# Three unread products ahead of the second half, and the scaled C moved ahead of a scan: a fused scan and gated feed-forward kernel on one core

## The chip, the cores and the metric

The kernel runs on 1 core of a Trainium2 chip. The metric is the device time of one execution in microseconds; medians of several executions are quoted. The engines are called by their short names: PE is TensorE (matmuls), PEld its weight loads, DVE is VectorE, ACT is ScalarE, POOL is GpSimd, SP issues the transfers. The span of a profile is about 1.7 us shorter than the time of the same execution.

## The reference, cut to what matters

The first half is a chunked linear recurrence over a sequence (4 sequences, 8 heads, 768 positions, head size 32, state size 16); the second multiplies its result (3072 x 256) by a matrix, applies h * cos(h), and multiplies by another.

```
y_intra = einsum('bhij,bhjd->bhid', (C @ B^T) * L, x)        # L: products of a, from j to i
y_inter = einsum('bhin,bhnd->bhid', C, state) * decay_to_i
state   = decay_full * state + sum_j (B_j x_j) * decay_from_j
...
h = x @ w_in ;  g = h * cos(h) ;  out = g @ w_out            # 256 -> 2048 -> 256
```

The weights arrive as 64-bit floats and are made into 32-bit floats in 16 pieces on the chip. Everything is computed in 32 bits.

## The kernel before

The sequence is cut into 6 blocks of 128 positions. One iteration n of the main loop handles one of 16 slices f of the feed-forward layer for one block c: `first(n)` makes hp (two matmuls of 128x512), ACT and DVE make k, w, the cosine and gT from it, `second(n-2)` adds four products into o. The scan of the next block is spread over the same iterations, one sequence b every three: `turn` transposes B and C, `intra` makes the products g and masks them with lam into m, `finish` makes y and the new state. Each matmul of the program stands in the trace as two instructions (hp: 384 for 192 calls), so hp is an x4 there and one unread product an x2. (1, 0) means block c = 1, sequence b = 0. In block 0's iterations the weights' conversion is there as well (`grade`, `join`), so block 1's scan, which runs beside it, is the most crowded part for DVE.

```python
def pair(name):                      # two buffers, passed round: tp, g, g, y, s_ps, ...
    return psum.tile([P, 2, 4 * P], FP32, tag="scan", bufs=2, name=name)

def decays(c, b, t):                 # lam: one scan of 128x512 per half t
    ...
    V.tensor_tensor_scan(out=lam[c, b][:, hs]..., data0=rows_, data1=unit, ...)
    if t == 0:
        return
    if c > 0:
        reach[c, b] = r = scan.tile([P, P], FP32, tag="reach", bufs=2, name="reach")
        V.tensor_tensor_scan(out=r, data0=along[c][:, b], data1=ones, initial=1.0, ...)
    ...
    G.tensor_tensor(out=sc, ...)     # POOL

def turn(c, b, tag=None):
    ...                              # PE: transposes of B and C into tp
    for t in range(2):
        ACT.activation(cT[:, t], tp[:, 1], AF.Copy, scale=slot[:, t:t + 1])
    ACT.copy(out=bcT[:, 0], in_=tp[:, 0])
    if c > 0:                        # the scaled C: last reader of tp
        V.tensor_tensor(out=bcT[:, 1], in0=tp[:, 1], in1=reach[c, b], op=ALU.mult)

def finish(c, b, tag=None, fills=0):
    ...
    fill(y[:, 2:4], fills)           # products of ones that nothing reads
    ...
def join(which, i):                  # last steps of a weight piece
    V.tensor_scalar(out=bits, ...)
    V.scalar_tensor_tensor(out=bits, in0=high, ..., in1=bits, ...)
    G.tensor_tensor(out=dst, in0=bits, in1=last, op=ALU.add)   # POOL, two inputs
...
    # in the loop, for the next block's sequence b:
    if j == 0:
        decays(c + 1, b, 1)          # lam's second half, reach
    (turn, intra, finish)[j](c + 1, b)
```

Of the kernel before, what the change touches and what calls it, by code (L numbers as in the profile page):

```python
# [8 lines left out]
FP32 = mybir.dt.float32  # L9
# [3 lines left out]
ALU = mybir.AluOpType  # L13
# [12 lines left out]
def kernel(  # L26
# [23 lines left out]
    V, ACT, G, PE = nc.vector, nc.scalar, nc.gpsimd, nc.tensor  # L50
# [3 lines left out]
    P = 128  # L54
    NC = S // P
# [13 lines left out]
    scan = ctx.enter_context(tc.tile_pool(name="scan", bufs=2))  # L69
# [9 lines left out]
    def bank(shape, name, tag):  # L79
        return psum.tile(shape, FP32, tag=tag, bufs=2, name=name)  # L80

    def pair(name):

        return psum.tile([P, 2, 4 * P], FP32, tag="scan", bufs=2, name=name)


    raw, arow, along = {}, {}, {}
    ones = const.tile([P, P], FP32, name="ones")
    V.memset(ones, 1.0)

    def fill(dst, times=1):

        for _ in range(times):
            PE.matmul(dst, lhsT=ones, rhs=ones.unsqueeze(1).to_broadcast([P, dst.shape[1], P]),
                      start=True, stop=True, skip_group_check=True)
# [27 lines left out]
    def load_along(c):  # L123
# [11 lines left out]
        out=a_in, in_=a.rearrange("(u b) h (c p) -> (b h c) u p", u=NU, p=P))  # L135
# [25 lines left out]
    def grade(which, i, later=False):  # L161



        t = words.pop((which, i), None)
        if t is None:
            return
        low, high = t[:, :, 0], t[:, :, 1]
        mag = conv.tile([P, 2 * WC], FP32, tag="mag", bufs=3, name="mag")
        ACT.activation(mag, high.bitcast(FP32), AF.Abs)  # L170
        G.tensor_scalar(out=mag, in0=mag, scalar1=MOST, scalar2=LEAST,  # L171
                        op0=ALU.min, op1=ALU.max)
        last = conv.tile([P, 2 * WC], U32, tag="last", bufs=3, name="last")
        held[which, i] = (high, mag.bitcast(U32), last)

        def rest():
            ACT.activation(last, low, AF.Copy, scale=2.0 ** -29)
        if later:
            return rest
        rest()  # L180

    def join(which, i):



        if (which, i) not in held:
            return
        high, bits, last = held.pop((which, i))
        V.tensor_scalar(out=bits, in0=bits, scalar1=3, scalar2=0x3FFFFFFF,  # L189
                        op0=ALU.logical_shift_left, op1=ALU.bitwise_and)  # L190
        V.scalar_tensor_tensor(out=bits, in0=high, scalar=0xC0000000, in1=bits,  # L191
                               op0=ALU.bitwise_and, op1=ALU.bitwise_or)
        dst = kept(which, i)
        k = dst.shape[1]
        G.tensor_tensor(out=dst.bitcast(U32), in0=bits.rearrange("p (k f) -> p k f", k=k),
                        in1=last.rearrange("p (k f) -> p k f", k=k), op=ALU.add)
# [3 lines left out]
    for n in (0, 2, 1, 3, 4, 5):  # L200
# [14 lines left out]
                    fill=0.0, base=0, channel_multiplier=1)  # L215
    G.affine_select(out=own, in_=own, pattern=[[N, H], [0, D]], compare_op=ALU.is_ge,
                    fill=0.0, base=N - 1, channel_multiplier=-1)
# [18 lines left out]
    scaled, lam, reach, state, part, yT = {}, {}, {}, {}, {}, {}  # L236

    def heads(b):
        return slice(b * H, (b + 1) * H)
# [3 lines left out]
    def spread_a(b, tags):  # L243
# [3 lines left out]
        for t in range(2):  # L247
# [4 lines left out]
                          rhs=cut[:, u], start=(h == 0), stop=True, skip_group_check=True)  # L252
            spread[b].append(a_ps)

    def decays(c, b, t):


        if t == 0:
            lam[c, b] = scan.tile([P, H, P], FP32, tag="lam", bufs=3, name="lam")
        hs = slice(t * HH, (t + 1) * HH)  # L260
        rows_ = spread[b][t] if c == 0 else arow[c, b][:, hs]
        V.tensor_tensor_scan(  # L262
            out=lam[c, b][:, hs].rearrange("p h i -> p (h i)"),
            data0=rows_.rearrange("p h i -> p (h i)"),
            data1=unit.rearrange("p h i -> p (h i)"), initial=0.0,
            op0=ALU.mult, op1=ALU.add)
        if t == 0:
            return
        if c > 0:
            reach[c, b] = r = scan.tile([P, P], FP32, tag="reach", bufs=2, name="reach")  # L270
            V.tensor_tensor_scan(out=r, data0=along[c][:, b], data1=ones, initial=1.0,
                                 op0=ALU.mult, op1=ALU.mult)
        if c == NC - 1:
            return

        scaled[c, b] = sc = scan.tile([P, H, N], FP32, tag="sc", bufs=NB, name="sc")
        G.tensor_tensor(out=sc, in0=raw[c][0][:, 0, heads(b)],  # L277
                        in1=lam[c, b][:, :, P - 1:P].to_broadcast([P, H, N]), op=ALU.mult)
# [33 lines left out]
    def finish(c, b, tag=None, fills=0):  # L312
        (bcT, m), xr = part.pop((c, b)), raw[c][1]
        y = (pair("y")[:, 0] if tag is None else bank([P, 4 * P], "y", tag)
             ).rearrange("p (k i) -> p k i", k=4)
        fill(y[:, 2:4], fills)
        y = y[:, 0:2]
        if c > 0:
            s = state[c - 1, b].rearrange("p h d -> p (h d)")
            for t in range(2):  # L320
                PE.matmul(y[:, t], lhsT=s[:, t * P:(t + 1) * P], rhs=bcT[:, 1],  # L321
                          start=(t == 0), stop=False, skip_group_check=True)
        for h in range(H):
            q, t = h % 4, h // 4
            PE.matmul(y[32 * q:32 * q + 32, t], lhsT=xr[:, b, h], rhs=m[:, h],  # L325
                      start=(c == 0 and t == 0), stop=True, tile_position=(0, 32 * q),
                      skip_group_check=True)
        if b == 0:
            yT[c] = two.tile([P, 2, TB], FP32, tag="yT", name="yT")
        ACT.copy(out=yT[c][:, :, b * P:(b + 1) * P], in_=y)  # L330
        if c > 0:
            carry(c, b)

    def carry(c, b):

        if c == NC - 1:
            return
        xr, sc = raw[c][1], scaled.pop((c, b))
        s_ps = pair("s_ps")[:, 0, 0:2 * D]
        for q in range(4):  # L340
            two_ = slice(2 * q, 2 * q + 2)
            PE.matmul(s_ps[32 * q:32 * q + 32], lhsT=sc[:, two_].rearrange("p h n -> p (h n)"),  # L342
                      rhs=xr[:, b, two_].rearrange("p h d -> p (h d)"), start=True, stop=True,
                      tile_position=(0, 32 * q), skip_group_check=True)
        state[c, b] = new = states.tile([P, H, D], FP32, tag="state", name="state")
        by_two = "p (k t) d -> p k (t d)"
        V.tensor_tensor(out=new.rearrange(by_two, k=HP),
                        in0=s_ps.unsqueeze(1).to_broadcast([P, HP, 2 * D]),
                        in1=own.rearrange(by_two, k=HP), op=ALU.mult)
        if c > 0:  # L350
            V.scalar_tensor_tensor(out=new, in0=state.pop((c - 1, b)),
                                   scalar=reach[c, b][:, P - 1:P], in1=new,
                                   op0=ALU.mult, op1=ALU.add)


    hp, turns, gT, o = {}, {}, {}, {}
# [14 lines left out]
    def gate(n):  # L371
        cos = turns.pop(n)
        ACT.activation(cos, cos, AF.Sin, bias=quarter, scale=TWO_PI)  # L373
        gT[n] = ffn.tile([P, TB], FP32, tag="gT", bufs=LAG + 1, name="gT")
        V.tensor_tensor(out=gT[n], in0=hp.pop(n), in1=cos, op=ALU.mult)  # L375
# [26 lines left out]
    fill(bank([P, 4, P], "warm", "o"), 2)  # L402
    spread_a(0, ("h", "h"))
    decays(0, 0, 0)
    decays(0, 0, 1)
    spread_a(1, ("o", "o"))
    turn(0, 0)
# [19 lines left out]
    finish(0, 2, "o", 1)  # L427
    intra(0, 3)
    grade(*order[1])
    finish(0, 3, "o")  # L430
    join(*order[2])
    join(*order[1])
    load(1)
# [9 lines left out]
    for n in range(NC * NF + LAG):  # L443
        c, f = divmod(n, NF)
        rest = None
        if n < NC * NF:
            if f == 0 and c > 0:
                load(c + 2)
            first(n)
            if n + 3 < len(order):  # L450
                rest = grade(*order[n + 3], later=True)
            if n + 2 < len(order):
                join(*order[n + 2])
            gate(n)
            if rest:
                rest()
        if n >= LAG:
            second(n - LAG)
        if n < NB:
            carry(0, n)  # L460
        if c + 1 < NC:
            b, j = divmod(f - 3, 3)
            if 0 <= b < NB:
                if j == 0:
                    decays(c + 1, b, 1)
                (turn, intra, finish)[j](c + 1, b)
            b, j = divmod(f - 2, 3)
            if 0 <= b < NB and j == 0:
                decays(c + 1, b, 0)
            if f == NF - 1:  # L470
                raw.pop(c + 1)
                load_a(c + 2)
                load_along(c + 2)
# [30 lines left out]
```

## Time and profile before

| | before |
|---|---|
| time, median of 5 | 414.45 us (413.12 to 414.99) |
| span of the profile | 413.0 us |
| PE busy | 403.4 us (98%) |
| DVE busy | 269.7 us (65%) |
| ACT, POOL busy | 174.6, 42.8 us |
| granted clock, mean | 0.995 |

The table hides two things. The mean clock of 0.995 comes of one stretch of 3.4 us at half rate (0.50 from 23.05 to 26.46 us), and of 0.9 us more at the end of the span (0.50 from 412.17 us on), behind the last matmul. And 98% for PE is a count of time in which some matmul is in flight, so g counts as busy for all of its 1.34 us in block 1, though it takes 0.71 in block 2 and the rest is its second half waiting for a buffer. In the lines that follow, "L303" is line 303 of the kernel, and the lines of the changed kernel are one lower.

### The profile page before, as it was taken

The page shows a single profiled execution, that of the slowest core. Times are in us where ns is not written, and L with a number is a line of the kernel's source. Part 1 is how long each engine was busy: PE and PEld are TensorE (multiplying, and loading weights), DVE is VectorE, ACT ScalarE, POOL GpSimd, SP SyncE. Part 2 cuts the span into 40 slices and gives each one's busy share as a digit, 9 for nine tenths or more (in the row PEclk, how much of TensorE's full clock was granted, in tenths as well). Part 3 has the DMA queues.
Part 4 walks back from the last instruction along what each step waited for, and adds up shares of the span by engine and source line. Part 5 has one row for each costly group of instructions (what it writes and reads, how often), then busy time and mean ns, then how long its engine had stood idle before and what let it go on. Part 6 is the DMA issues. An engine that isn't in the chain of part 4 may idle for free.

```text
span 413.0 us, 5500 instructions
## 1 busy us (share of the span) xinstructions
PE 403.4 (98%) x2088; PEld 263.4 (64%) x2088; DVE 269.7 (65%) x410; ACT 174.6 (42%) x329; POOL 42.8 (10%) x62
## 2 busy tenths in 40 slices
PE   8979999999999999999999999999999999999995
PEld 5636665666666666666666666667666666666664
DVE  5979999964777664676764667674576664444442
ACT  2457575634344334443343433433443443433331
POOL 2265455410000000000000000000000000000000
PEclk9989999999999999999999999999999999999999
DMA  7999994092110164201146111120100000100001
GB/s 92 312 146 305 389 148 141 2 160 70 52 51 2 51 116 64 97 6 51 52 94 86 51 52 51 51 60 19 52 0 2 0 0 2 51 0 2 0 0 52
DMA packets 105978, 30.27 MB, mean 73 GB/s; under 512 B 75168, under 2 KB 101856, under 8 KB 105952
## 3 DMA queue, kind: packets, MB, share of 16 engines
q1 hardware_dynamic: 105952, 29.92, 30.7%
q8 instruction: 16, 0.26, 0.3%
q14 instruction: 10, 0.08, 0.1%
HBM read 26.57 MB, written 3.34 MB: 72 GB/s over the span
## 4 chain that ended last, share of the span: by engine, by line
PE 89%; SPq 5%; DVE 3%; DMA 2%; issue 0%; ACT 0%; DVEq 0%
PE hp L362 40%; PE o L386 39%; SPq L112 4%; PE g L303 4%; PE y L325 3%; PE y L321 2%; DMA words<-in_moe_w_in_dram 1%; DMA along<-a_all 1%; DVE mag L191 1%; PE tp L284 1%; PE tp L285 1%; DVE lam L262 0%; DVE mag L189 0%; PE s_ps L342 0%; DVE gT L375 0%
## 5 line engine op out<-in xcount | busy, mean ns | idle before, releaser
L362 PE MATMUL hp<-yT,w_in 128*128 128x512 f32 x384 | 186.6, 609 | 1.2 <-ACT yT L330 0.6
L386 PEld LDWEIGHTS o<-w_out,gT 128*128 128x128 f32 x768 | 145.9, 190 | 60.0 <-issue 44.0
L386 PE MATMUL o<-w_out,gT 128*128 128x256 f32 x768 | 181.1, 379 | 0.0
L366 ACT ACTIVATE k<-hp 128x512 int32<-128x512 f32 x96 | 57.3, 597 | 129.9 <-PE hp L362 129.9
L375 DVE TENSOR_TENSOR gT<-hp,w 128x512 f32<-128x512 f32 x96 | 66.2, 690 | 65.4 <-ACT w L373 65.4
L368 DVE SCALAR_TENSOR_TENSOR w<-hp,k 128x512 f32<-128x512 f32 x96 | 66.1, 689 | 63.0 <-ACT k L366 62.3
L362 PEld LDWEIGHTS hp<-yT,w_in 128*128 128x128 f32 x384 | 68.3, 191 | 58.7 <-issue 54.3
L373 ACT ACTIVATE w<-w,quarter 128x512 f32<-128x512 f32 x96 | 69.3, 722 | 76.3 <-DVE w L368 76.3
L262 DVE TENSOR_TENSOR_SCAN lam<-arow,unit 128x512 f32<-128x512 f32 x40 | 51.4, 1286 | 0.0
L307 DVE TENSOR_TENSOR m<-g,lam 128x512 f32<-128x512 f32 x48 | 30.7, 680 | 0.7 <-PE g L303 0.6
L277 POOL TENSOR_TENSOR sc<-bc,lam 128x128 f32<-128x128 f32 x20 | 8.2, 412 | 201.5 <-DVE lam L262 200.2
L303 PE MATMUL g<-cT,bcT 32*128 32x256 f32 x192 | 19.7, 426 | 1.9 <-ACT bcT L291 1.2
L289 ACT ACTIVATE cT<-tp,slot 128x128 f32<-128x128 f32 x48 | 14.6, 355 | 11.0 <-PE tp L285 11.0
L325 PE MATMUL y<-m,xr 128*32 128x128 f32 x384 | 15.9, 279 | 1.1 <-DVE m L307 1.1
L303 PEld LDWEIGHTS g<-cT,bcT 32*128 32x128 f32 x192 | 8.6, 183 | 10.8 <-issue 6.2
L191 DVE SCALAR_TENSOR_TENSOR mag<-words,mag 128x512 uint32<-128x512 uint32 x16 | 14.3, 894 | 0.5
L330 ACT COPY yT<-y 128x256 f32<-128x256 f32 x24 | 9.0, 374 | 11.6 <-PE y L325 11.5
L171 POOL TENSOR_SCALAR mag<-mag 128x512 f32<-128x512 f32 x16 | 12.2, 759 | 16.3 <-ACT mag L170 16.3
L321 PEld LDWEIGHTS y<-bcT,state 128*128 128x128 f32 x80 | 12.1, 191 | 1.0
L325 PEld LDWEIGHTS y<-m,xr 128*32 128x32 f32 x384 | 8.9, 109 | 5.3 <-DVE m L307 2.4
L321 PE MATMUL y<-bcT,state 128*128 128x128 f32 x80 | 12.2, 274 | 0.0
L170 ACT ACTIVATE mag<-words 128x512 f32<-128x512 f32 x16 | 10.8, 677 | 2.1 <-DMA words<-in_moe_w_in_dram 2.1
(43 smaller groups left out, 152.1 us busy)
## 6 DMA issues: line engine op xcount, KB each, us to landing
arow<-a_cut SPq DMA_DIRECT2D x20, 512.0 KB
words<-in_moe_w_in_dram SPq DMA_DIRECT2D x8, 512.0 KB
words<-in_moe_w_out_dram SPq DMA_DIRECT2D x8, 512.0 KB
xr<-in_x_dram SPq DMA_DIRECT2D x5, 512.0 KB
out_dram<-ob SPq DMA_DIRECT2D x10, 256.0 KB
bc<-in_B_dram SPq DMA_DIRECT2D x5, 256.0 KB
bc<-in_C_dram SPq DMA_DIRECT2D x5, 256.0 KB
along<-a_all SPq DMA_DIRECT2D x20, 64.0 KB
```

The source lines that it names most:

```text
L191: V.scalar_tensor_tensor(out=bits, in0=high, scalar=0xC0000000, in1=bits, op0=ALU.bitwise_and, op1=ALU.bitwise_or)
L262: V.tensor_tensor_scan(out=lam[c, b][:, hs].rearrange("p h i -> p (h i)"), data0=rows_.rearrange("p h i -> p (h i)"), data1=unit.rearrange ...
L303: PE.matmul(g[u // 2][:, u % 2, 0:2 * P], lhsT=bcT[r, 0], rhs=cT[r].rearrange("p t i -> p (t i)"), start=True, stop=True)
L307: V.tensor_tensor(out=m[:, hs].rearrange("p (k t) i -> p k (t i)", k=2), in0=g[u][:, :, 0:2 * P], in1=l[:, hs].rearrange("p (k t) i -> p k ...
L321: PE.matmul(y[:, t], lhsT=s[:, t * P:(t + 1) * P], rhs=bcT[:, 1], start=(t == 0), stop=False, skip_group_check=True)
L325: PE.matmul(y[32 * q:32 * q + 32, t], lhsT=xr[:, b, h], rhs=m[:, h], start=(c == 0 and t == 0), stop=True, tile_position=(0, 32 * q), skip ...
L362: PE.matmul(hp[n], lhsT=w_in[:, k, f * P:(f + 1) * P], rhs=yT[c][:, k], start=(k == 0), stop=(k == KT - 1))
L366: ACT.activation(k, hp[n], AF.Copy, bias=0.25, scale=INV_2PI)
L368: V.scalar_tensor_tensor(out=w, in0=hp[n], scalar=INV_2PI, in1=k, op0=ALU.mult, op1=ALU.subtract)
L373: ACT.activation(cos, cos, AF.Sin, bias=quarter, scale=TWO_PI)
L375: V.tensor_tensor(out=gT[n], in0=hp.pop(n), in1=cos, op=ALU.mult)
L386: PE.matmul(o[c][b // 2][:, b % 2], lhsT=g[:, b * P:(b + 1) * P], rhs=w_out[:, f], start=(f == 0 and (last or b % 2 == 0)), stop=(f == NF ...
```

## The change

It aims at both: more work for PE around the last y of block 0, so that its clock, 0.50 there for 3.4 us, is not lowered just ahead of the main loop, and the scaled C earlier on DVE, so that the products g find their buffer free. reach, which the scaled C needs, is made in the iteration before.

```diff
+    def reaches(c, b):
+        reach[c, b] = r = scan.tile([P, P], FP32, tag="reach", bufs=2, name="reach")
+        V.tensor_tensor_scan(out=r, data0=along[c][:, b], data1=ones, initial=1.0, ...)
     def decays(c, b, t):
...
-        if c > 0:
-            reach[c, b] = ...            # moved to reaches()
...
-    finish(0, 3, "o")
+    finish(0, 3, "o", 2)
+    fill(pair("warm")[:, 0, 0:2 * P].rearrange("p (k i) -> p k i", k=2), 1)
...
             if 0 <= b < NB:
+                (turn, intra, finish)[j](c + 1, b)
                 if j == 0:
                     decays(c + 1, b, 1)
-                (turn, intra, finish)[j](c + 1, b)
             b, j = divmod(f - 2, 3)
             if 0 <= b < NB and j == 0:
+                reaches(c + 1, b)
                 decays(c + 1, b, 0)
```

More of the change, by code (lines that the diff above doesn't have):

```diff
@@ L253, in spread_a @@
             spread[b].append(a_ps)
+    def reaches(c, b):
+        reach[c, b] = r = scan.tile([P, P], FP32, tag="reach", bufs=2, name="reach")
+        V.tensor_tensor_scan(out=r, data0=along[c][:, b], data1=ones, initial=1.0,
+                             op0=ALU.mult, op1=ALU.mult)
     def decays(c, b, t):
@@ L266, in decays @@
             op0=ALU.mult, op1=ALU.add)
-        if t == 0:
-            return
-        if c > 0:
-            reach[c, b] = r = scan.tile([P, P], FP32, tag="reach", bufs=2, name="reach")
-            V.tensor_tensor_scan(out=r, data0=along[c][:, b], data1=ones, initial=1.0,
-                                 op0=ALU.mult, op1=ALU.mult)
-        if c == NC - 1:
+        if t == 0 or c == NC - 1:
             return
```

## The prediction

That the clock would hold rests on the estimate from two windows of the profile before, one with PE busy 2.03 of 3.41 us (60%) ahead of the drop and one with 2.63 of 3.42 us (77%) without one. The 0.43 us of one unread product is an estimate as well, from o's products in the same trace: eight instructions of 128x256, two to a product, take 1.73 us from their first start to that of the next instruction (45.22 to 46.95 us) and 1.89 us to their own end.

> **What bounds the kernel now.** I read the page first, then the stretches of time, then the timeline and the landings of the transfers in the first 90 us. On the page PE is busy 403.4 of 413.0 us, and its tenths show where the rest is: a ramp at the start and a short tail.
>
> ```profile
> PE   8979999999999999999999999999999999999995
> PEclk9989999999999999999999999999999999999999
> ```
>
> The third digit of the clock row, an 8, is the first thing the change aims at. The matmul timeline around it (start, duration, engine, line, shape, in brackets the idle time before and its releaser):
>
> ```profile
> 20.23 0.71 PE L303 MATMUL g<-cT,bcT 32*128 32x256 f32 x8
> 21.72 0.42 PE L325 MATMUL y<-m,xr 128*32 128x128 f32 x8 [0.78 <-DVE m L307]
> 22.32 0.43 PE L325 MATMUL y<-m,xr 128*32 128x128 f32 x8 [0.17 <-DVE m L307]
> 23.32 3.51 PE L362 MATMUL hp<-yT,w_in 128*128 128x512 f32 x4 [0.58 <-ACT yT L330]
> 27.01 1.98 PE L362 MATMUL hp<-yT,w_in 128*128 128x512 f32 x4
> ```
>
> The last y of block 0 stands between idle times of 0.78, 0.17 and 0.58 us, and the first product of the second half (hp, n = 0) then takes 3.51 us where the next takes 1.98. The granted clock is 0.80 in 20 to 25 us and 0.85 in 25 to 30 us, that is (0.20 + 0.15) * 5 / 0.5 = 3.5 us at half rate.
>
> The second thing is hidden: PE counts as busy from 29.8 us on, but not all of that is work. Stretches of one scan step (three n) in block 1 and in block 2 (columns: PE, PEld, DVE, ACT, POOL busy, clock, DMA share, GB/s):
>
> ```profile
> 43.40:56.75 13.35, 13.35 (x76) 8.64 (x75) 13.11 (x21) 8.44 (x17) 6.54 (x7) 1.00 1.12 307
> 56.75:70.10 13.35, 13.35 (x76) 8.64 (x75) 13.11 (x21) 8.45 (x17) 6.56 (x7) 1.00 0.57 126
> 70.10:83.45 13.35, 13.35 (x76) 8.64 (x74) 13.11 (x21) 7.87 (x16) 5.97 (x6) 1.00 0.14 38
> 109.95:122.67 12.72, 12.72 (x79) 8.35 (x75) 9.12 (x14) 4.80 (x11) 0.41 (x1) 1.00 0.14 43
> ```
>
> The same matmuls take 13.35 us in block 1 and 12.72 us in block 2. In block 1 DVE is busy 13.11 of 13.35 us, since the weights' joins run beside the scan. The 0.63 us stand in one place, the g products:
>
> ```profile
> 53.44 1.91 DVE L262 TENSOR_TENSOR_SCAN lam<-arow,unit 128x512 f32<-128x512 f32 x1
> 55.28 0.39 DVE L271 TENSOR_TENSOR_SCAN reach<-along,ones 128x128 f32<-128x128 f32 x1
> 55.48 1.34 PE L303 MATMUL g<-cT,bcT 32*128 32x256 f32 x8
> 55.77 0.29 DVE L293 TENSOR_TENSOR bcT<-tp,reach 128x128 f32<-128x128 f32 x1
> ```
>
> g takes 1.34 us here and 0.71 in block 2. Its second half needs the PSUM pair of tp (two buffers, passed round), whose last reader is the scaled C (bcT), which stands behind lam and reach on DVE. For b = 0 it is worse: g's halves start at 41.38 and 42.77 us, and the next hp at 43.40 instead of 41.38 + 0.65 = 42.03, a loss of 1.37. From block 2 on PE has no hole; DVE has 3.6 us to spare per step.
>
> [...] here the longest gap is 0.78, and the drop followed a window (19.59 to 23.00) with PE busy only 2.03 of 3.41 us, while 2.63 of 3.42 (9.35 to 12.77) kept the clock. [...] lam from arow takes 1.21 us alone and 1.91 when w_in's last join on POOL (53.00 to 54.27) overlaps it; the join on DVE 0.69 or 0.98. [...]
>
> **The change part by part.** In block 0 it adds three unread products of 256 columns: two ahead of the last y, one behind. One takes about 0.43 us of the array (the existing ones: 0.60 with latency). The first two fill 20.94 to 21.80, and m is ready at 21.62, so they cost at most 0.1; the third lies in the 0.58 us in which PE waits for ACT's yT. Cost on the path about 0. Busy time in the window rises from 2.03 to about 3.2 of 3.41, so the clock should hold, and hp (n = 0) ends 1.6 us sooner (3.51 - 1.9). Through k (ACT 0.60), w (DVE 0.69), sin (ACT 0.72) and gT (DVE 0.69) that reaches the third hp, which waited for gT at 29.82: about 28.2 now.
>
> In the loop, no instruction is added or removed, four stand elsewhere: scaled C (0.29) goes ahead of lam's second half (1.21 to 1.91) and no longer right behind reach, and reach (0.39) moves to the step before. What I get by placing the measured durations one after the other:
> - The copies of a for (1, 0) land at 35.36 us and the seventh weight piece at 37.08, by the landings in the trace; neither depends on compute. lam's first half started at 35.87 and can start at 35.4 at the earliest: DVE gains only 0.45 there, not 1.6. sin (n = 3) stands behind the seventh piece's first step on ACT (37.17 to 37.85).
> - That lam then misses most of the POOL join that lengthened it to 1.59, and the other half likewise; so w (n = 4) comes at about 41.5, not 42.63. DVE gains 1.1.
> - Scaled C also waits for ACT's copy of the same tile, which ends at about 40.0 (last 0.67, cT 0.60, bcT 0.27 after sin). So g starts at about 40.05 in one piece, not at 41.38 in two, and the next hp at 40.8, not 43.40.
> - The y of (1, 0) then waits for m, at about 45.0 (46.17 before): hp (n = 6) at 45.8, not 48.17. PE gains 2.3 to 2.5.
> - For b = 1 to 3, PE can gain 0.63 more each, up to 2.5 + 1.9 = 4.4. But it must not outrun DVE: before, m was done 1.3 to 1.5 us before y needed it. With DVE ahead by 1.1 the limit is 2.6. DVE gains a little per step: lam's second half now comes after ACT's copy, when the POOL join is nearly over (up to 0.6 saved), the bubble of 0.1 between reach and scaled C is gone; against this it waits up to 0.4 for ACT, and reach pushes lam's first half into the next POOL operation (0.3). I take 0 to 0.5 per step, hence a limit at b = 3 between 2.6 and 4.1.
>
> Blocks 2 to 5: PE has no hole to fill. In the step with reach DVE is 0.39 us later, but gT has over 2 us of slack before hp needs its bank. Nothing there.
>
> Sum: 2.6 to 4.1, middle 3.3. 414.45 - 3.3 = 411.15; I say 411.2.
>
> **Rivals.**
> A: DVE is the bound of block 1 and gives nothing but order. Its instructions are the same, 13.11 of 13.35 us busy, so only the initial slack of 1.5 us is gained, and the hole reappears at y (waiting for m). For it: the busy share. Against: part of those 13.11 us is time blocked by POOL, which the new order avoids. Time: 412.5 to 413.
> B: The clock does not hold, or drops one or two windows later. For it: once hp (n = 1) ends at 27.1, PE waits until 28.2 for gT, 1.1 us in the window of 26.4 to 29.8: 68% busy, between the two shares seen. Against: most of that loss falls where transfers hold DVE anyway (35.36 and 37.08 us). It costs 0 to 1: 411.2 to 412.2.
> C: Everything is hidden: transfers set when block 1 begins. For it: the landings. Against: holes of 1.37 + 3 * 0.63 = 3.26 us in g come from DVE's order, not from a transfer. Time: 414.
> D: PE takes all it can (1.6 + 3.26 less a short wait for ACT): 4.4, giving 410.0.
> E: The wait of scaled C for ACT holds up DVE in all 20 steps and slows blocks 2 to 5. For it: the built program has that wait, and lam no longer covers it. Against: DVE is busy only 9.12 of 12.72 us there. Time if it did: 413 to 415.
>
> **Range and chances.** The middle is 411.2. A and B together pull towards 412.5, D towards 410.2; I put 8 in 10 on 410.2 to 412.7. Faster by over 2% would be below 406.2, more than every hole of PE after 20 us together; slower by over 2% would need over 8 us of new waits. So within 2% is nearly certain.
>
> **What would show it right or wrong.** The clock row should have no 8 in its third digit and the first hp should take about 1.98 us. The g products of block 1 should take about 0.71 us each, g of (1, 0) starting near 40 us, and a step of block 1 between 12.7 and 13.1 us. lam's second half should mostly take less than 1.9 us. Block 2's step should stay at 12.72 us; if it is longer, E holds. If block 1's step stays near 13.3 with the wait now at y, A holds. If g of (1, 0) still starts after 41 us, the transfers or the clock have taken the gain and my working from 35 us on is wrong.

## The result, and the profile after

The changed kernel takes 410.12 us (median of 5, 409.48 to 410.62) against 414.45. The ratio is 0.990, with a 95% interval of 0.988 to 0.992. Ratios here are the mean time of one kernel's fast executions over that of the other's in the same rounds, so not quite the ratio of the medians; in the last call of the experiments, 11 of the 12 executions of the kernel before are those of the first call, on the same chip. The gain of 4.3 us is clear of the noise. The median lies 0.08 us under the low end of the predicted range.

The tenths of PE's busy time and of its clock, 40 slices of the span, after:

```profile
PE   8999999999999999999999999999999999999995
PEclk9999999999999999999999999999999999999999
```

The 7 (PE) and the 8 (clock) of the third slice are gone. The matmul timeline around block 0's last y, after:

```profile
20.57 0.71 PE L302 MATMUL g<-cT,bcT 32*128 32x256 f32 x8
21.21 1.13 PE L94 MATMUL y<-ones 128*128 128x256 f32 x4
22.27 0.81 PE L324 MATMUL y<-m,xr 128*32 128x128 f32 x16
23.02 0.70 PE L94 MATMUL warm<-ones 128*128 128x256 f32 x2
23.67 1.95 PE L361 MATMUL hp<-yT,w_in 128*128 128x512 f32 x4
25.80 1.98 PE L361 MATMUL hp<-yT,w_in 128*128 128x512 f32 x4
28.61 1.96 PE L361 MATMUL hp<-yT,w_in 128*128 128x512 f32 x4 [0.57 <-DVE gT L374]
```

The unread products stand where PE waited, nothing else moved for them, and the first hp takes 1.95 us. From g to hp it is 3.10 us (20.57 to 23.67), before 3.09 (20.23 to 23.32), so they cost nothing. The third hp still waits 0.57 us for gT, but it starts at 28.61, not 29.82.

The steps of block 1 and one of block 2, after (columns: PE, PEld, DVE, ACT, POOL busy with the number of instructions, clock, DMA share, GB/s):

```profile
40.82:53.54 12.72, 12.72 (x78) 8.36 (x74) 12.22 (x22) 8.20 (x16) 6.54 (x7) 1.00 1.13 358
53.54:66.26 12.72, 12.72 (x78) 8.36 (x74) 12.23 (x21) 8.20 (x16) 6.47 (x8) 1.00 0.83 148
66.26:78.98 12.72, 12.72 (x78) 8.36 (x74) 12.21 (x21) 7.64 (x15) 6.45 (x8) 1.00 0.14 43
105.48:118.20 12.72, 12.72 (x79) 8.35 (x75) 9.11 (x15) 5.00 (x10) 0.41 (x1) 1.00 0.14 42
```

A step of block 1 now takes exactly what one of block 2 takes, 12.72 us. DVE is busy 0.9 us less per step (12.22, was 13.11) with the same instructions. Where the 0.9 went is seen in the timeline of the step of b = 1, after:

```profile
51.12 1.27 POOL L195 TENSOR_TENSOR w_in<-mag,last 128x512 uint32<-128x512 uint32 x1 [1.32 <-DVE mag L191]
51.99 0.29 DVE L292 TENSOR_TENSOR bcT<-tp,reach 128x128 f32<-128x128 f32 x1 [0.36 <-ACT bcT L290]
52.20 1.27 DVE L267 TENSOR_TENSOR_SCAN lam<-arow,unit 128x512 f32<-128x512 f32 x1
52.90 0.71 PE L302 MATMUL g<-cT,bcT 32*128 32x256 f32 x8
```

The scaled C waits 0.36 us for ACT's copy, lam starts when POOL's join (51.12 to 52.39) is nearly over and takes 1.27 us instead of 1.91, and g finds its buffer free.

The ledger, from the starts of hp in the two traces:

| stretch | before | after | gain |
|---|---|---|---|
| start to hp of n = 0 | 23.32 | 23.67 | -0.35 |
| n = 0 to n = 1 (clock) | 3.69 | 2.13 | 1.56 |
| n = 4 to n = 5 (g of b = 0) | 5.56 | 4.18 | 1.38 |
| n = 7 to 8, 10 to 11, 13 to 14 (g of b = 1 to 3), each | 4.81 | 4.18 | 0.63 |
| sum of the last three rows, the last of them taken three times | | | 4.83 |

With the later start the net is 4.5 us; the spans differ by 4.4 (413.0 and 408.6). The later start lies ahead of anything that was changed.

The chain that ended last says the same by engine, first before, then after:

```profile
PE 89%; SPq 5%; DVE 3%; DMA 2%; issue 0%; ACT 0%; DVEq 0%
```

```profile
PE 97%; ACT 1%; DVE 1%; issue 0%; DVEq 0%
```

Before, the chain left PE at g of (1, 0) and ran back over DVE to the transfers; after, it is PE nearly all the way.

### The profile page after: what moved, and what is told of

The parts are those of the page before. It is cut to its first block, busy times and chain, and to the rows that moved or that the text cites. A ratio compares the mean times of both kernels' runs of the same rounds, so it can differ in the third digit from the quotient of the medians.

```text
span 408.6 us, 5540 instructions
## 1 busy us (share of the span) xinstructions
PE 401.1 (98%) x2094; PEld 263.1 (64%) x2094; DVE 266.7 (65%) x410; ACT 173.8 (43%) x329; POOL 42.3 (10%) x62
## 4 chain that ended last, share of the span: by engine, by line
PE 97%; ACT 1%; DVE 1%; issue 0%; DVEq 0%
PE hp L361 42%; PE o L385 41%; PE g L302 4%; PE y L324 3%; PE y L320 2%; PE a_ps L251 2%; PE warm L94 1%; PE tp L283 1%; PE tp L284 1%; PE s_ps L341 1%; PE y L94 0%; ACT cT L288 0%; ACT w L372 0%; DVE m L306 0%; DVE gT L374 0%
## 5 line engine op out<-in xcount | busy, mean ns | idle before, releaser
L267 DVE TENSOR_TENSOR_SCAN lam<-arow,unit 128x512 f32<-128x512 f32 x40 | 48.6, 1214 | 0.0
L302 PE MATMUL g<-cT,bcT 32*128 32x256 f32 x192 | 17.1, 426 | 1.2 <-ACT bcT L290 1.2
L191 DVE SCALAR_TENSOR_TENSOR mag<-words,mag 128x512 uint32<-128x512 uint32 x16 | 13.4, 840 | 0.6
L302 PEld LDWEIGHTS g<-cT,bcT 32*128 32x128 f32 x192 | 7.5, 182 | 8.7 <-issue 6.5
```

The lines of the kernel that those rows point to most:

```text
L267: V.tensor_tensor_scan(out=lam[c, b][:, hs].rearrange("p h i -> p (h i)"), data0=rows_.rearrange("p h i -> p (h i)"), data1=unit.rearrange ...
L302: PE.matmul(g[u // 2][:, u % 2, 0:2 * P], lhsT=bcT[r, 0], rhs=cT[r].rearrange("p t i -> p (t i)"), start=True, stop=True)
```

## The experiments

Twelve runs of nine different kernels were made, four to a call, each call on one chip with runs of the kernel before. On these chips the kernel before had medians of 415.2 us, 0.7 to 0.8 above the first comparison, while the changed kernel kept its time; why is not known, so the kernels below are compared by ratio. All gave correct results.

The mean clock of every execution, profiled or not, tells whether there was a stretch at half rate. One of 3.41 us lowers the mean to 0.996 or less (3.41 * 0.5 / 409 = 0.004). The four fast profiles with such a stretch have 0.994 to 0.996; the nine fast ones without have 0.998 to 1.000, what is missing there was read as a lower clock behind the last matmul, as in the kernel before (last matmul ended at 408.65 us, clock 0.50 from 412.17 us on).

### The unread products alone

```diff
-    finish(0, 3, "o")
+    finish(0, 3, "o", 2)
+    fill(pair("warm")[...], 1)          # the loop in its old order
```

> The kernel before with the three unread products alone, the loop in its old order. Both theories: no half-rate stretch, the first hp takes about 1.95 us instead of 3.51, the third hp starts near 28.5 us. Theory PE-sum (every hole of PE that goes is worth its full size): 1.6 us faster, 412.9. Theory DVE-bound (block 1 is set by DVE in the old order, which starts block 1 when the copies of a have landed): the steps of block 1 stay at 13.35 us, g still takes 1.34, and the gain is only what DVE gains at its first lam, 0.4 to 1.2 us: 413.3 to 414.1.

The five undisturbed executions took 413.05 to 414.97 us, ratio 0.997 (0.995 to 1.000). The profiled one was slow: 521.45 us, granted clock 0.754 over the whole span. It tells nothing of the change.

> The unread products alone in the old order, again, since the profile of the first try fell in a state with the clock at 0.75. Expected of a fast profile: no half-rate stretch, first hp about 1.95 us, g of block 1 still 1.34 us in steps of 13.35. Time 0.5 to 1.2 us below before, as the first try's fast runs (ratio 0.9973) have it.

Median 414.38 against 415.22, ratio 0.997 (0.994 to 1.000), profile with no stretch at half rate. Its g of (1, 0), and a step of block 1:

```profile
40.11 0.70 PE L303 MATMUL g<-cT,bcT 32*128 32x256 f32 x4
41.50 0.29 DVE L293 TENSOR_TENSOR bcT<-tp,reach 128x128 f32<-128x128 f32 x1
41.85 0.70 PE L303 MATMUL g<-cT,bcT 32*128 32x256 f32 x4 [1.04 <-DVE bcT L293]
```

```profile
55.83:69.17 13.34, 13.34 (x76) 8.63 (x74) 13.10 (x21) 8.44 (x17) 6.56 (x7) 1.00 0.81 140
```

The first hp is at full rate and PE arrives at g 1.3 us sooner than before (40.11, was 41.38), and then waits longer for the same scaled C: from g's start to the next hp it is 2.37 us, was 2.02. The steps stay at 13.34. So in the old order part of the clock's gain is lost at that wait, as the DVE-bound theory said. Another part is lost because the products alone do not always keep the clock: of the 11 undisturbed executions of both tries four have a mean clock of 0.994 to 0.996 (414.87 to 416.27 us), seven 0.997 to 1.000 (413.05 to 414.80 us). Where the four had their stretch is not on record; the join off POOL, below, shows a place.

### The order alone

```diff
-    finish(0, 3, "o", 2)
-    fill(pair("warm")[...], 1)
+    finish(0, 3, "o")                   # the loop in its new order
```

> The changed kernel without the three unread products: the new order alone. The clock drops as in the kernel before and the first hp takes about 3.5 us. Theory PE-sum: the holes of g go in full (1.37 + 3 * 0.63 = 3.26 us), steps of block 1 take 12.72 us, time 411.2. My prediction's limit by DVE: g is whole but y waits for m, steps of block 1 near 13.0 to 13.3, gain 1.5 to 2.5, time 412 to 413. If the drop's loss is hidden once the holes are gone, time 410.1 as in the changed kernel.

Median 409.89 against 415.21, ratio 0.988 (0.986 to 0.991). In the profile the clock drops as before, and all four g take 0.71 us in steps of 12.72 us. The first hp and the window ahead of the drop:

```profile
23.39 3.54 PE L361 MATMUL hp<-yT,w_in 128*128 128x512 f32 x4 [0.58 <-ACT yT L329]
```

```profile
19.77:23.18 3.41, 1.92 (x32) 0.79 (x32) 3.24 (x7) 2.90 (x7) 2.71 (x3) 1.00 1.22 223
```

The holes of g go in full, also without the products, so DVE did not hold PE back here as I had expected. (PE comes to block 1 later in this execution than in the changed kernel's, hp of n = 5 at 42.13 against 40.82 us, so it is the changed kernel's steps of 12.72 us that show it for a PE that gains everything.) But the median is 1.3 us below what the full gain of the order alone should give (411.2), nearly the changed kernel's. The single times explain it: 409.45, 409.54, 409.88, 409.89, and 411.39, 411.86; the profiled one is the 411.39. So I formed a new theory: the drop comes in some executions only.

> The order alone, again. Of its six first times four were 409.45 to 409.89 and two 411.39 and 411.86, and the profiled one of the two had the half-rate stretch. Theory of a drop in some executions: again two clusters about 1.6 to 2.0 us apart, the lower one within 0.5 of the changed kernel; the median is then that of the commoner cluster. Theory that the products always gain 1.6: one cluster near 411.7.

Times 410.13 and 410.56, and 411.31, 411.81, 411.97, 412.01; median 411.56. This time the profiled one is of the lower cluster (410.56), and its clock did not drop. Its windows on the grid of the clock records (their limits lie whole multiples of 3.413 us apart: in the kernel before at 23.05, 26.46 and 412.17 us, so 1 and 113 of them; that the grid goes on between two limits is an estimate, and counted on from this profile's limits it has points at 18.21, 21.63 and 25.04):

```profile
18.21:21.63 3.42, 2.31 (x34) 0.79 (x33) 3.29 (x7) 3.35 (x8) 1.90 (x2) 1.00 1.08 341
21.63:25.04 3.41, 2.82 (x21) 1.25 (x22) 3.34 (x4) 0.77 (x3) 2.41 (x3) 1.00 0.94 96
```

The matmuls are the same and so are the holes, but here the grid cuts through them: PE is busy 2.31 and 2.82 us in two windows. Where one window held nearly all of the holes, at 1.92 us (the order alone, first try) or 1.98 us (the kernel before, 19.64 to 23.05), the clock fell. Over both tries six times lie in 409.45 to 410.56 and six in 411.31 to 412.01. Two of the twelve executions were profiled, one of each cluster, with and without the drop. The clocks show that the other ten split in the same way: all six of the upper cluster have 0.994 to 0.996, all six of the lower 0.998 to 1.000.

The same reading for all executions in the fast state:

| kernel | with a stretch at half rate (clock 0.996 or less) | without (0.997 or more) |
|---|---|---|
| before | 23 of 23: 414.18 to 417.95 us | none |
| products alone | 4 of 11: 414.87 to 416.27 | 413.05 to 414.80 |
| order alone | 6 of 12: 411.31 to 412.01 | 409.45 to 410.56 |
| changed kernel | 0 of 15 | 409.45 to 411.37 |

Five executions of the kernel before have a clock of 0.990, by estimate about 8 us at half rate (0.010 * 415 / 0.5) and so more than one stretch of 3.41; they are its five slowest (417.00 to 417.95 us). Neither half of the change keeps the clock in every execution, both together did in all 15.

> The changed kernel unaltered, on one chip with the order alone. Theory that the unread products only take away a drop of the clock that comes in some executions: all runs near 410.1 us, in one cluster (spread under 1.2), no half-rate stretch in the profile. Theory that they always gain 1.6: its median lies 1.6 below that of the order alone.

Times 409.92, 410.29, 410.34, 410.35, and 411.16, 411.37; ratio 0.987 against 0.989 for the order alone, about 0.8 us. So the median is where it should be, but the spread (1.45) is wider than expected (under 1.2). The profiled execution is the one of 411.16, at full clock throughout. Its lateness comes from elsewhere:

```profile
36.43 1.22 DVE L267 TENSOR_TENSOR_SCAN lam<-arow,unit 128x512 f32<-128x512 f32 x1 [1.77 <-DMA arow<-a_cut]
40.74 0.81 PE L302 MATMUL g<-cT,bcT 32*128 32x256 f32 x8 [1.31 <-DVE state L346]
```

lam waited 1.77 us for its rows, and PE stood 1.31 us ahead of g. So the landing of block 1's first transfers is a second thing that varies from one execution to the next: the rows of (1, 0) were there at 34.57 us in the first profile of the changed kernel, at 36.40 here and at 35.33 in the third. In this profile and the third the first step of block 1 takes 13.08 us, not 12.72, as y of (1, 0) waits for m.

### Parts of the order

reach one step earlier, and the scaled C still behind lam:

```diff
                 if j == 0:
                     decays(c + 1, b, 1)
                 (turn, intra, finish)[j](c + 1, b)
             ...
+                reaches(c + 1, b)
                 decays(c + 1, b, 0)
```

> No unread products; reach in the preceding scan step, but scaled C still behind lam's second half. Scaled C comes 0.39 us plus a bubble of 0.1 earlier within its step than before, but DVE still has lam (up to 1.91 us, blocked by POOL) ahead of it, and lam's first half comes 0.39 later. Theory that the place of lam matters: the hole of g shrinks by at most 0.5 us per step at first, but the step stays DVE-bound near 13.3 us: gain 0 to 1.0, time 413.4 to 414.4. If reach was what mattered: g near 0.71 and gain over 2 us.

Median 413.19, ratio 0.994 (0.992 to 0.997); steps of 13.02 us, g 1.40 us for b = 0 and 1.01 to 1.02 after. That is a gain of 2.0 us, more than I had expected (0 to 1.0): the step does shrink by 0.33 us when reach stands elsewhere.

The scaled C ahead of lam, and reach right ahead of it in the same step:

```diff
+                if j == 0:
+                    reaches(c + 1, b)
                 (turn, intra, finish)[j](c + 1, b)
                 if j == 0:
                     decays(c + 1, b, 1)
```

> No unread products; scaled C ahead of lam's second half, reach right ahead of scaled C in the same step. Theory that the place of lam matters: g is whole (0.71 us), steps of block 1 near 12.72 us, gain nearly that of the order alone: 411.2 to 411.8. If it takes reach's move as well: scaled C waits 0.5 us more in each step and the gain is under half of the order's: over 412.8.

Median 411.49, ratio 0.992 (0.989 to 0.994): more than the other part, less than both. Steps of 12.95 us, g 1.47 us for b = 0, 0.76 to 0.77 for the rest. By their clocks five of six executions of the kernel with reach early had a stretch at half rate, and two of six of this one; among those that had one the order is the same (412.86 to 413.55 us, 412.58 and 412.69, and 411.31 to 412.01 for the order alone). The timeline of b = 1 shows what reach is doing there:

```profile
51.35 1.27 POOL L195 TENSOR_TENSOR w_in<-mag,last 128x512 uint32<-128x512 uint32 x1 [1.31 <-DVE mag L191]
51.78 1.11 DVE L258 TENSOR_TENSOR_SCAN reach<-along,ones 128x128 f32<-128x128 f32 x1
53.00 0.29 DVE L292 TENSOR_TENSOR bcT<-tp,reach 128x128 f32<-128x128 f32 x1
```

reach takes 1.11 us instead of 0.39: now it is what stands behind POOL's join, and the scaled C waits for it. In both orders it is the scan right behind gT that meets the join (lam with 1.91 us before, reach with 1.11 here). In the changed kernel the scaled C stands there, and it took 0.28 to 0.29 us inside POOL's joins (at 39.33, 51.99, 64.54 and 77.11 us) and 0.29 in block 2, where POOL has none (at 102.45 us). One of its inputs is in PSUM; whether that is the reason was not shown.

### The join off POOL

If that is so, the old order without POOL's join should not have the holes either.

```diff
-        G.tensor_tensor(out=dst.bitcast(U32), in0=bits..., in1=last..., op=ALU.add)
+        def place():                    # called behind the iteration's other ACT work
+            ACT.copy(out=dst, in_=bits.bitcast(FP32)...)
```

> The kernel before (old order, no unread products) with the last step of each weight's join made by a ScalarE copy instead of GpSimd's add: the low bits of the weights are dropped on purpose, an error near one part in a million, so the result may still count as correct. DVE's instructions are the same. Theory POOL-block [...]: lam's second half takes about 1.21 us instead of 1.91, steps of block 1 fall to 12.7 to 12.9, g for b = 1 to 3 near 0.71, time 1.5 to 2.5 us below before. Theory of order alone (scaled C is late because it stands behind lam): g still takes over 1.2 us, time within 0.6 of before.

Median 412.60 against 415.22, ratio 0.993 (0.989 to 0.997), though the profiled execution had a stretch at half rate at another place (43.08 to 46.49 us; the hp there takes 3.09 us, not 1.98), and by their clocks (0.992 to 0.996) the other five had one too. It came behind this window, in which PE waits for g of (1, 0):

```profile
39.66:43.07 3.41, 2.06 (x10) 1.09 (x11) 3.27 (x7) 2.67 (x8) 1.02 (x2) 1.00 1.08 376
```

So the old order has a second place at which the clock can fall. The gain of 2.6 us is a little above the expected range. lam takes 1.20 to 1.23 us in all eight cases of block 1. A step of block 1:

```profile
69.47:82.19 12.72, 12.72 (x78) 8.36 (x74) 12.32 (x21) 9.45 (x19) 2.18 (x3) 1.00 0.13 40
```

12.72 us in the old order, and g takes 0.71 us for b = 1 to 3. Its g for b = 0 still has a hole (1.85 us from start to end). So for b = 1 to 3 the hole was DVE blocked by POOL (lam 1.91 us beside the join, 1.20 to 1.23 with the join off POOL), and the change removes it by moving the scan out of the way. For b = 0 a hole stays without the blocking: the scaled C (41.36 us) stands behind a lam of 1.22 us, and PE, already through with the first half of g, waits for it. That part is one of order.

### How near DVE is to the bound

```diff
                 if j == 0:
                     decays(c + 1, b, 1)
+                    if c == 0:
+                        more(c + 1, b)   # one more scan of 128x512, its result unread
```

> The changed kernel with one more scan of 128x512 (about 1.2 us, its result unread) on VectorE behind lam's second half in each of block 1's four steps. Theory that VectorE runs just ahead of TensorE in block 1 (m ends 0.5, 0.7, 0.8 and 1.3 us before y needs it): 4.8 us of added work less 1.3 of slack, 3.3 to 3.7 us slower than the changed kernel, steps of block 1 near 13.7 us with y waiting for m. Theory that VectorE has room in block 1 (the ACT wait and idle time take it up): under 1.5 us slower.

Median 413.01, 3.1 us over the changed kernel (409.90); a step:

```profile
54.52:68.05 13.53, 12.99 (x79) 8.28 (x75) 13.02 (x22) 8.09 (x16) 7.19 (x7) 1.00 0.74 134
```

Four scans of 1.19 us (4.8 us in all) cost 3.1: a little less than expected, and the step is 13.53, not 13.7. So block 1 of the changed kernel has about 1.7 us of DVE work to spare over its four steps and no more. m's second half ends every 12.55 us in the changed kernel's trace (44.65, 57.20, 69.75), against PE's 12.72.

### Fewer products, other loads

Two products ahead of y, none behind it:

```diff
     finish(0, 3, "o", 2)
-    fill(pair("warm")[...], 1)
```

> The changed kernel without the third unread product, the one behind the last y. The two ahead fill the hole of 0.78 us and leave 0.17 and 0.58, so PE is busy some 2.8 of 3.41 us. Theory of the busy share (kept at 77%, dropped at 60%): the clock holds, times as the changed kernel within 0.3. If the product behind is needed: a second cluster about 1.5 us above, as with the order alone.

Median 409.65 (409.50 to 410.37), ratio 0.987, one cluster, with clocks of 0.999 and 1.000: as the changed kernel. Five executions can't exclude a rare drop, but nothing shows that the product behind y is needed.

> The changed kernel unaltered, as the measure for the others of this call. 409.9 to 411.4, median 410.3.

Median 409.90 (409.45 to 409.97, 4 executions), ratio 0.987.

The rows for reach of b = 1 to 3 loaded behind the copies of a:

```diff
-    load_along(1)
+    load_along(1, (0,))
     for b in range(NB):
         load_a(1, (b,))
+        if b > 0:
+            load_along(1, (b,))
```

> The changed kernel with the rows for reach of sequences 1 to 3 of block 1 loaded later, each behind its copies of a, so that the copies for (1, 0) and the seventh weight piece land sooner (each of the three took about 0.6 us of landings). Theory that what is left to vary in the changed kernel is the landing of (1, 0): lam's first half of (1, 0) starts by 35.1 us, g of (1, 0) is whole, no wait of y for m, time 409.6 to 410.1, with fewer executions over 411. Theory that PE is already dense: the same time as the changed kernel within 0.3.

Median 409.44 (409.24 to 410.26), ratio 0.9865 against 0.9870 for the changed kernel: not told apart. lam of (1, 0) starts at 35.37 us, as it did in the first profile of the changed kernel, since reach ahead of it took 0.79 us (0.41 in the later steps of the changed kernel). So in an execution where the transfers are in time, PE is dense already. Whether this version helps in those where they are late is open: only one of its five was profiled, and none took over 410.3 us.

## Why the prediction was right or wrong

**What bounds the kernel** held: PE, with holes in two places, at the sizes read from the profile before. The sum of the holes that went is 4.83 us in the ledger, against 1.6 + 3.26 = 4.86 that I had read out. One reading was off: PE does not count as busy all the time from 29.8 us on. Of the loss at g of (1, 0), 0.69 us ahead of 42.77 count as idle; only the rest was hidden.

**The products** did what was predicted: no cost, hp of n = 0 at 1.95 us (1.9), the clock held. For the kernel before, the drop that I took from one profile is the rule, with all 23 later executions below 0.997. What the prediction didn't see is that in the new order it is a matter of chance: the products then gain about 1.6 us in the one kind of execution and nothing in the other, 0.5 to 0.8 us on average by the ratios (0.9883 and 0.9887 for the order alone, 0.9870 and 0.9867 for both). Nor did it see that in the old order the products alone don't always keep the clock (4 of 11 had a stretch). Its estimate from the busy share, kept at 77% and dropped at 60%, is too simple as well. Around y and g the clock fell after windows of the grid with PE busy 1.92, 1.98 and 2.06 of 3.41 us (56% to 60%: the order alone, the kernel before, the join off POOL) and held after 2.31 and 2.82 (68% and 83%, the order alone again). But at the end of the changed kernel, where the work is o alone, it held at 1.00 to the end of the span (408.6 us) after a window with PE busy 1.56 of 3.42 us (402.62 to 406.04, 46%). So the busy share alone does not tell when the clock falls; what does was not shown.

**The first step of block 1** came out within a few tenths: g at 40.05, it was 40.18; the next hp at 40.8, it was 40.82; m at 45.0, it was 44.65; hp of n = 6 at 45.8, it was 45.59. For g this was in part luck. My working had the transfers land as before, so that g would wait for ACT's copy until about 40.0. In fact the seventh weight piece landed at 36.01 us (37.09 before), the copy ended at 39.13, and g started at 40.18 because PE, busy with o until then, came no sooner. The rows of (1, 0) landed at 34.57 us (35.36 before), but reach, which took 0.79 us with POOL's join beside it (33.89 to 35.16), kept lam at 35.37. And DVE gained 1.5 us in this step (m ready at 44.65, was 46.16), where I had 1.1.

**The term that was mis-sized** is "I take 0 to 0.5 per step", DVE's gain in each of the steps b = 1 to 3, and with it the limit of 2.6 to 4.1 (the 0.4 us more from the first step raise it as well, but less). The mechanism was right (PE must not outrun m, and POOL's blocking is what the order can save), the size was too small. DVE's period went from 13.35 to 12.55 us, 0.80 per step. From the durations in the two traces: lam's second half 1.91 to 1.27 (0.64; I had "up to 0.6"); the weights' joins on DVE 0.98, 0.98, 0.69 before and 0.69, 0.69, 0.98 after (0.29; not in my sum); the bubble between reach and scaled C (0.1); less the wait for ACT (0.36; "up to 0.4"). The 0.3 that I had put against it for lam's first half was not there: it takes 1.19 us. That makes 0.67; the other 0.13 I can't assign. At 0.80 DVE keeps ahead of PE, so PE took all of 3 * 0.63.

**The rivals.** A (DVE gives nothing but order) fell: the steps are 12.72 us, and with the join off POOL even the old order reaches that. But A is near: m's period of 12.55 us against 12.72 leaves 0.17 us per step, and the added scan found 1.7 us in all four steps. In two of the three profiles of the changed kernel the first step does wait for m, 0.36 us. B (a drop one or two windows later) did not come in any of the seven profiles of kernels with the products that were fast, though by their clocks four executions of the products alone had a drop somewhere. In the window I had feared PE waits 0.57 us, not 1.1, and is busy 2.83 of 3.40 us. C (hidden by transfers) fell as a whole, though lam waited for its rows in two of the three profiles of the changed kernel (1.77 and 0.67 us). D (PE takes all it can, 410.0) is what happened. E (the wait for ACT slows blocks 2 to 5) fell: 12.72 us there, DVE busy 9.11.

**The range** was pulled up by A and B, which both fell; that is why the median came out at its low edge.

## What to carry to other kernels

A PE that counts as fully busy can still hold waits (the steps of 13.35 and of 12.72 us both have PE busy throughout): compare the length of the same group of matmuls in two stretches of the kernel. Where DVE seems full, compare the durations of one instruction in several places before calling it the bound; some of its busy time may be lost to GpSimd (lam 1.91 us beside its join, 1.21 without), and putting the scaled C in the way of the collision (0.28 to 0.29 us in it and out of it), rather than a scan, gave it back here. And a stretch at half clock in one profile is one draw: several times, looked at one by one with the clock of each, tell whether it is the rule.
